# A decode step of gated attention and MLP: four groups of TensorE products turned from written-out code into loops with register addresses

## The chip, the cores and the metric

The kernel runs on one core of one Trainium2 chip. The metric is the device time of one execution in microseconds (us). Times of engine work below come from one profiled execution of the kernel, whose clock starts with the span. TensorE is called PE, and its weight loads PEld; VectorE is DVE, ScalarE ACT, GpSimd POOL, SyncE SP. Each engine has a sequencer that works through its own program in order. Instructions that the sequencer does itself (register arithmetic, branches, waits) are shown by the trace with their own names: FUSED_REGOPS, ALU_OP, MOVE, COMPARE_BRANCH, EVENT_SEMAPHORE.

## The reference

One token (x of 512 elements, bf16) goes through two branches, which are mixed by a gate:

```python
q = (x @ wq).reshape(B, Sq, H, Dh).transpose(0, 2, 1, 3)      # H = 32 heads, Dh = 128
scores = einsum("bhqd,bhkd->bhqk", q, k_cache) * (Dh ** -0.5)  # Sk = 65536 keys for each head
p = softmax(scores, axis=-1)
o = einsum("bhqk,bhkd->bhqd", p, v_cache)
a = o.transpose(0, 2, 1, 3).reshape(B, Sq, H * Dh) @ wo

b = (silu(x @ w_gate) * (x @ w_up)) @ w_down                   # 512 -> 1792 -> 512

g = sigmoid((x * gate_w).sum(-1, keepdims=True))
out = g * a + (1 - g) * b
```

K and V caches have 32 x 65536 x 128 bf16 elements each, 1074 MB together. All weights together are 14 MB.

## The kernel before

Every cache element is used once, so the kernel streams K and V through one large SBUF buffer `mem` (184 slots of 512 elements for each of the 128 partitions). For one head, K and V are each loaded in two halves (z = 0 and 1) of 8.39 MB. A partition holds R = 512 keys of a head.

**SP's queue (L214 to 252)** issues almost all loads, in an order written out by hand. Ahead of the block, wq and the weights of gate, up and down are issued (L205 to 207). Then come the two quarters of K's first half of head 0 (L221, 222). SP then waits for `s_q`, the end of the products with wq (L224), since the second half of K of head 0 goes into the slots of wq (V0). After that, for each head h: K's first half of head h once enough transposes are done (L227; for h = 1 eight of them, `NP`), V's first half of head h - 1 (for h = 1 after 13 transposes and after `s_b`, the end of the MLP's down product; later after a part of the V products), K's second half, V's second half. At the end come wo (L240) and the V of the last head in eight pieces (`tail`, L61: 128, 128, 128, 64, 32, 16, 12 and 4 rows), each with a semaphore `dt_[n]` of its own, and two last parts of wo (L249, 250).

**DVE (L318 to 432)** first serves the small head of the computation: x transposed, q in the layout that the scores want (L377 to 382), and the MLP's activation up to `guT` (L383 to 389). Then it transposes K by 32 x 32 blocks into the two buffers of `kt` (`transposes`, L336; in the head loop L405 and L412), each transpose waiting for the scores that used the same buffer two before (`qkdone`). It also spreads the exponentials for the V products (`shuffle`, L345).

**ACT** does the exponentials (L307) and small copies; among them qcur (L289) and gcol (L291, `s_gc`), one behind the other.

**PE (L434 to 585)**, in order:

- x transposed by four products (L440).
- The products with wq (L444 to 447): for each of 32 heads four products over c accumulate one column of psM. The last one raises `s_q`.
- q spread by `sel` (L452), the gate's broadcast (L456).
- `mlp_up` (L467 to 478): it waits for `s_gc` and the gate's and up weights; for each of 14 columns j, four products with wg and four with wu, 112 in all. The last one raises `s_h`.
- The down product (L481 to 484, 14 products of 512 columns).
- The head loop `Fori(0, H)` (L494 to 536): scores of head i in pairs of transposed blocks, and between them the V products of head i - 1. `scores` (L458) is written for 32 products; `pieces` runs pairs in a loop over j with `ds(j * (2 * PR) + o, 4)` as output address, or once with fixed addresses.
- After the loop: `turn` (L487), then `piece(0)` (128 products of one column into psW, L544), the gathering of the heads' outputs (L554, oR by DVE at L426), 31 products with wo (L558 to 560, 512 columns each, into psY; the last raises `s_y`), `piece(1)`, four small products with `hot` (L567), `piece(2)` to `piece(7)`, the last raising `s_w`, and the last products of wo (L583). ACT's copy (L314) and two writes of 0.5 KB end the kernel.

In `piece`, the weights of a product are a row block `vt[:, r * Dh:(r + 1) * Dh]` and the moving operand is one column `pb[:, col]`. For the first piece, k_col[r] is r.

Of the kernel before, what the change touches and what calls it, by code (L numbers as in the profile page):

```python
# [15 lines left out]
ds = bass.DynSlice  # L16
# [5 lines left out]
def bass_gated_mix__mha_block_cached__swiglu_ffn__decode_kernel(  # L22
# [11 lines left out]
    out: bass.AP,  # L34
):
    _, H, S, Dh = A_k_cache.shape
    D = A_wq.shape[0]
    F = B_w_gate.shape[1]
    Dc = D // P
    FC = F // P  # L40
    R = S // P
# [12 lines left out]
    k_col = [256 * z + PR * k_order[z].index(r // PR) + r % PR for z in range(2) for r in range(HR)]  # L54
# [10 lines left out]
    with ExitStack() as ctx:  # L65
        def sb(name, shape, dt):
            return ctx.enter_context(nc.sbuf_tensor(name, shape, dt))

        def psum(name, shape, dt):
            return ctx.enter_context(nc.psum_tensor(name, shape, dt))  # L70

        def sem(name):
            return ctx.enter_context(nc.semaphore(name))
# [3 lines left out]
        psY = psum("psY", [P, 512], F32)  # L77
        psM = psum("psM", [P, 512], F32)
        psQ = psum("psQ", [P, 4, 128], F32)
        psT = psum("psT", [P, 512], F32)  # L80
        psW = psum("psW", [P, 512], F32)
# [7 lines left out]
        pb = sb("pb", [P, 512], BF16)  # L89
# [7 lines left out]
        xTb = sb("xTb", [P, 16], BF16)  # L97
# [7 lines left out]
        oR = sb("oR", [P, 32], BF16)  # L105
# [3 lines left out]
        def at(kb, n):  # L109
            return mem[:, kb * KB:kb * KB + n]  # L110
# [32 lines left out]
        s_h = sem("s_h")  # L143
# [45 lines left out]
        wq_ap = at(WQ, Dc * H * Dh).rearrange("p (c n) -> p c n", c=Dc)  # L189
# [3 lines left out]
        wo_ap = at(WO, 32 * D).rearrange("p (j n) -> p j n", j=32)  # L193
# [241 lines left out]
        def _(pe):  # L435
# [3 lines left out]
            for c in range(Dc):  # L439
                last = nc.tensor.matmul(psM[:, c:c + 1], xv[:, c, :], ones[0:1, 0:1], start=True, stop=True)  # L440
            last.then_inc(s_xT, 1)
            pe.wait_ge(s_xTb, 1)
            pe.wait_ge(d["wq"], 16)
            for h in range(H):  # L444
                for c in range(Dc):
                    last = nc.tensor.matmul(psM[:, 128 + h:129 + h], wq_ap[:, c, h * Dh:(h + 1) * Dh],  # L446
                                            xTb[:, c:c + 1], start=(c == 0), stop=(c == Dc - 1))
            last.then_inc(s_q, 1)
            pe.wait_ge(s_qTb, 1)
            pe.wait_ge(s_sel, 1)  # L450
            for je in range(4):
                last = nc.tensor.matmul(psQ[:, je, 0:H], sel[:, je, :], qTb[:], start=True, stop=True)  # L452
# [14 lines left out]
            def mlp_up():  # L467
                pe.wait_ge(s_gc, 1)
                pe.wait_ge(d["wg"], 16)
                pe.wait_ge(d["wu"], 16)  # L470
                for j in range(FC):
                    for w, o in ((wg_ap, 64), (wu_ap, 80)):
                        for c in range(Dc):
                            last = nc.tensor.matmul(psM[:, o + j:o + j + 1], w[:, c, :, j], xTb[:, c:c + 1],  # L474
                                                    start=(c == 0), stop=(c == Dc - 1))
                last.then_inc(s_h, 1)

            mlp_up()
            pe.wait_ge(d["wd"], 16)
            pe.wait_ge(s_gu, 1)  # L480
            for j in range(FC):  # L481
                last = nc.tensor.matmul(psY[0:1, :], guT[:, j:j + 1], wd_ap[:, j, :],
                                        start=(j == 0), stop=False)
# [10 lines left out]
            with nc.tensor.Fori(0, H) as i:  # L494
                n = i * (2 * NP)
# [42 lines left out]
            def piece(n):  # L538
                kb, r0, nr = tail[n]
                pe.wait_ge(dt_[n], 16)  # L540
                vt = at(kb, nr * Dh)
                for r in range(nr):
                    col = k_col[r0 + r]
                    last = nc.tensor.matmul(psW[:, 0:1], vt[:, r * Dh:(r + 1) * Dh], pb[:, col:col + 1],  # L544
                                            start=(r0 + r == 0), stop=(r0 + r == R - 1))
                return last

            pe.wait_ge(s_or, H)
            turn()
            pe.wait_ge(s_pba, H)  # L550
            piece(0)
            pe.wait_ge(s_A, 1)
            pe.wait_ge(s_b0, 5)
            nc.tensor.matmul(psQ[:, 0, 0:32], amat[:].rearrange("p h q -> p (h q)"), bmat[:],  # L554
                             start=True, stop=True).then_inc(s_R, 1)
            pe.wait_ge(s_oR, 1)
            pe.wait_ge(d["wo"], 16)
            for j in range(31):  # L558
                last = nc.tensor.matmul(psY[0:1, :], oR[:, j:j + 1], wo_ap[:, j, :], start=False, stop=(j == 30))
            last.then_inc(s_y, 1)  # L560
            piece(1)
            pe.wait_ge(s_yr, 1)
            pe.wait_ge(s_hot, 1)
            pe.wait_ge(s_zz, 1)
            zt = [psZ[32 * (c // 2):32 * (c // 2) + 2, 0:128] for c in range(4)]
            for c in (0, 2, 1, 3):
                nc.tensor.matmul(zt[c], hot[0:1, c % 2, :], yrow[0:1, 128 * c:128 * c + 128],  # L567
                                 start=(c % 2 == 0), stop=False)
            pe.wait_ge(s_pbz, H)
            piece(2)  # L570
            piece(3)
            piece(4)
# [5 lines left out]
            for e in range(2):  # L578
# [3 lines left out]
                for c in (0, 2, 1, 3):  # L582
                    last = nc.tensor.matmul(zt[c], w4[:, e, c % 2, :], w2_ap[:, e, c, :], start=False,  # L583
                                            stop=(e == 1 and c % 2 == 1))
# [29 lines left out]
```

## Time and profile before

| | |
|---|---|
| device time, median of 3 runs | 2518.57 us (2518.57 to 2519.21) |
| the profiled execution | 2518.66 us |
| its span | 2517.4 us |
| PE busy | 1675.3 us (67%), 21432 matmuls |
| PEld busy | 956.8 us (38%) |
| DVE busy | 1397.7 us (56%) |
| ACT, POOL busy | 65.6 us (3%), 26.8 us (1%) |
| granted TensorE clock, mean | 0.711 |
| DMA from HBM | 1087.77 MB |
| code loaded by queue q8 | 9 packets, 0.15 MB |

Busy shares are averages over the whole span; what decides is which wait ends last in a stretch. The chain of waits follows the work that ended last back from the last instruction. In a timeline row, the first number is the start, the second the time to the end of the group, and in brackets stands how long the engine had stood idle before and what ended that. In an answer for one source line, three numbers divided by strokes are the shortest, the median and the longest duration in ns, and PEldq stands for the sequencer of PE.

### The profile page before, as it was taken

How to read it: one execution, taken by the hardware profiler on the slowest of the kernel's cores; microseconds unless marked ns; L12 is line 12 of the kernel's file. 1: busy time of each engine (PE TensorE's matmuls, PEld its weight loads, DVE VectorE, ACT ScalarE, POOL GpSimd, SP SyncE). 2: the span in 40 equal slices, each digit the busy share in tenths (PEclk: the TensorE clock that was granted, in tenths of full speed). 3: DMA queues.
4: the chain of work that ended last, by engine and by line, in shares of the span. 5: the costliest groups of instructions: out<-in, count | busy, mean ns of one | idle time of the engine just before them, and what ended most of it. 6: DMA issues, size and time to landing. Idle time of an engine off the chain costs nothing.

```text
span 2517.4 us, 50622 instructions
## 1 busy us (share of the span) xinstructions
PE 1675.3 (67%) x21432; PEld 956.8 (38%) x21432; DVE 1397.7 (56%) x1631; ACT 65.6 (3%) x195; POOL 26.8 (1%) x83
## 2 busy tenths in 40 slices
PE   4566756667666577566676666766657756667667
PEld 3333333333433334333333333343333433333334
DVE  3764565554655645646456555465464564644653
ACT  0000000000000000000000000000000000000000
POOL 0000000000000000000000000000000000000000
PEclk8667767677677677676776767767767767677677
DMA  9999999999999999999999999999999999999999
GB/s 418 433 433 434 435 433 433 434 433 433 433 433 433 433 433 433 433 433 433 433 435 432 434 433 434 433 434 433 434 433 433 433 433 434 433 433 433 433 434 396
DMA packets 20474, 1087.97 MB, mean 432 GB/s; under 512 B 2282, under 2 KB 2668, under 8 KB 2924
## 3 DMA queue, kind: packets, MB, share of 16 engines
q1 hardware_dynamic: 20452, 1087.78, 99.9%
q8 instruction: 9, 0.15, 0.0%
q14 instruction: 5, 0.04, 0.0%
q10 hardware_dynamic: 8, 0.00, 0.0%
HBM read 1087.77 MB, written 0.00 MB: 432 GB/s over the span
## 4 chain that ended last, share of the span: by engine, by line
DMA 72%; PE 27%; DVE 0%; issue 0%; SPq 0%; ACT 0%
DMA mem<-in_A_v_cache_dram 70%; PE psO L515 27%; DMA mem<-in_A_k_cache_dram 2%; DMA mem<-in_A_wq_dram 1%; DVE kt L336 0%; PE psM L446 0%; SPq L247 0%; PE psZ L583 0%; PE psW L544 0%; ACT fin L314 0%
## 5 line engine op out<-in xcount | busy, mean ns | idle before, releaser
L462 PE MATMUL psS<-qcur,kt 128*128 128x4 bf16 x16384 | 573.7, 169 | 776.4 <-DVE kt L405 458.4
L515 PE MATMUL psO<-mem,pb 128*4 128x512 bf16 x3968 | 1033.6, 428 | 35.2 <-DMA mem<-in_A_v_cache_dram 35.2
L405 DVE STREAM_TRANSPOSE kt<-mem 128x2048 uint32<-128x2048 uint32 x248 | 551.2, 2280 | 571.9 <-DMA mem<-in_A_k_cache_dram 571.0
L462 PEld LDWEIGHTS psS<-qcur,kt 128*128 128x128 bf16 x16384 | 534.7, 106 | 852.4 <-issue 850.0
L412 DVE STREAM_TRANSPOSE kt<-mem 128x2048 uint32<-128x2048 uint32 x248 | 547.6, 2274 | 407.6 <-DMA mem<-in_A_k_cache_dram 407.6
L515 PEld LDWEIGHTS psO<-mem,pb 128*4 128x4 bf16 x3968 | 361.2, 93 | 666.2 <-issue 235.7
L345 DVE COPY pb<-pa 32x64 bf16<-32x64 bf16 x1024 | 233.5, 228 | 24.2 <-PE psO L515 9.5
L350 DVE TENSOR_REDUCE sm<-psS 128x1 f32<-128x512 f32 x32 | 22.1, 692 | 42.3 <-PE psS L462 42.3
L336 DVE STREAM_TRANSPOSE kt<-mem 128x2048 uint32<-128x2048 uint32 x16 | 35.4, 2277 | 16.9 <-DMA mem<-in_A_k_cache_dram 16.9
L280 POOL PARTITION_ALL_REDUCE sm<-sm x32 | 11.2, 351 | 2392.6 <-DVE sm L350 2392.6
L301 ACT ACTIVATE oTn<-psT,gcol 128x1 bf16<-128x1 f32 x31 | 8.2, 263 | 1063.2 <-PE psT L489 1063.2
L489 PE MATMUL psT<-unit,orow 4*128 4x1 f32 x256 | 33.5, 248 | 0.8 <-ACT orow L299 0.8
L299 ACT ACTIVATE orow<-psO,sm 4x512 f32<-4x512 f32 x31 | 21.0, 677 | 439.5 <-issue 439.5
L489 PEld LDWEIGHTS psT<-unit,orow 4*128 4x128 f32 x256 | 30.8, 186 | 1.9 <-ACT orow L299 1.3
L305 ACT ACTIVATE sm<-sm 128x1 f32<-128x1 f32 x32 | 6.5, 203 | 886.3 <-POOL sm L280 886.3
L307 ACT ACTIVATE pa<-psS,sm 128x512 bf16<-128x512 f32 x32 | 22.0, 687 | 1.0
L544 PE MATMUL psW<-pb,mem 128*128 128x1 bf16 x512 | 14.6, 165 | 7.6 <-DMA mem<-in_A_v_cache_dram 7.1
L544 PEld LDWEIGHTS psW<-pb,mem 128*128 128x128 bf16 x512 | 14.1, 102 | 8.7 <-issue 6.5
L282 POOL PARTITION_ALL_REDUCE sm<-sm x32 | 12.3, 383 | 36.4 <-ACT pa L307 36.4
L446 PE MATMUL psM<-xTb,mem 128*128 128x1 bf16 x128 | 3.6, 165 | 11.1 <-DMA mem<-in_A_wq_dram 11.1
L474 PE MATMUL psM<-xTb,mem 128*128 128x1 bf16 x112 | 6.9, 198 | 4.9 <-DMA mem<-in_B_w_up_dram 4.9
L432 DVE TENSOR_SCALAR w<-psW,sm 128x2 bf16<-128x2 f32 x1 | 0.2, 221 | 16.5 <-PE psW L544 16.5
(64 smaller groups left out, 63.1 us busy)
## 6 DMA issues: line engine op xcount, KB each, us to landing
mem<-in_A_v_cache_dram SPq DMA_DIRECT2D x3, 4096.0 KB, 29.4
mem<-in_A_k_cache_dram SPq DMA_DIRECT2D x2, 4096.0 KB, 38.8
mem<-in_A_wq_dram SPq DMA_DIRECT2D x1, 4096.0 KB, 12.6
mem<-in_A_wo_dram SPq DMA_DIRECT2D x1, 3968.0 KB, 37.0
mem<-in_A_v_cache_dram SPq DMA_DIRECT2D x1, 2048.0 KB, 32.9
mem<-in_B_w_gate_dram SPq DMA_DIRECT2D x1, 1792.0 KB, 16.4
mem<-in_B_w_up_dram SPq DMA_DIRECT2D x1, 1792.0 KB, 21.3
mem<-in_B_w_down_dram SPq DMA_DIRECT2D x1, 1792.0 KB, 25.1
```

Of the source, the lines that this page charges most:

```text
L282: nc.gpsimd.partition_all_reduce(Lt, rsum, P, RADD).then_inc(s_L, 1)
L299: nc.scalar.mul(orow[0:4, :], psO[0:4, :], Li[0:4, :]).then_inc(s_or, 1)
L307: nc.scalar.activation(pa[:], psS[:], ACT.Exp, bias=nbias, scale=SCALE, accum_out=rsum).then_inc(expdone, 1)
L336: nc.vector.transpose(kt[:, i % 2, :].rearrange("p (j r t) -> p r j t", j=2, t=32), src.rearrange("p (r j t) -> p r j t", j=2, t=32)).then ...
L345: last = nc.vector.tensor_copy(dst, sr)
L350: nc.vector.reduce_max(mxs, psS[:], AX_X).then_inc(s_mx, 1)
L405: nc.vector.transpose(kt[:, c % 2, :].rearrange("p (j r t) -> p r j t", j=2, t=32), src.rearrange("p (r j t) -> p r j t", j=2, t=32)).then ...
L412: nc.vector.transpose(kt[:, c % 2, :].rearrange("p (j r t) -> p r j t", j=2, t=32), src.rearrange("p (r j t) -> p r j t", j=2, t=32)).then ...
L462: last = nc.tensor.matmul(psS[:, o:o + 4] if j is None else psS[:, ds(j * (2 * PR) + o, 4)], ktb[b][:, je // 2, r, :, je % 2], qcur[:, je, ...
L489: last = nc.tensor.matmul(psT[:, 0:1], orow[0:4, i * Dh:(i + 1) * Dh], unit[0:4, i:i + 1], start=(i == 0), stop=(i == 3))
L515: last = nc.tensor.matmul(psO[0:4, :], pb[:, k_col[256 * z + r]:k_col[256 * z + r] + 4], vt[:, r * Dh:(r + 4) * Dh], start=(z == 0 and par ...
L544: last = nc.tensor.matmul(psW[:, 0:1], vt[:, r * Dh:(r + 1) * Dh], pb[:, col:col + 1], start=(r0 + r == 0), stop=(r0 + r == R - 1))
```

## The change

Four groups of PE products that Python wrote out one by one become loops of the PE sequencer. Inside a loop, the addresses come from registers (`ds(expression, size)`). The last products of a group stay written out (in the piece the first eight), because they carry the start or stop flags or the semaphore.

- wq: 7 turns of 4 heads (16 products each), then 4 heads written out.
- gate and up: 13 turns of one column j (8 products each), then the last column.
- the last V's first piece: 8 rows, then 15 turns of 8 rows. The other pieces stay written out.
- wo: 5 turns of 5 products, then 6 written out.

Number, order and operands of the products stay as they were; no load, wait or semaphore is added or moved.

```diff
-            for h in range(H):
+
+            def project(h):
                 for c in range(Dc):
-                    last = nc.tensor.matmul(psM[:, 128 + h:129 + h], wq_ap[:, c, h * Dh:(h + 1) * Dh],
+                    last = nc.tensor.matmul(psM[:, ds(h + 128, 1)], wq_ap[:, c, ds(h * Dh, Dh)],
                                             xTb[:, c:c + 1], start=(c == 0), stop=(c == Dc - 1))
+                return last
+
+            with nc.tensor.Fori(0, (H - 4) // 4) as i:
+                for h in range(4):
+                    project(i * 4 + h)
+            for h in range(H - 4, H):
+                last = project(h)
             last.then_inc(s_q, 1)
...
-                for j in range(FC):
+                def up(j):
                     for w, o in ((wg_ap, 64), (wu_ap, 80)):
                         for c in range(Dc):
-                            last = nc.tensor.matmul(psM[:, o + j:o + j + 1], w[:, c, :, j], xTb[:, c:c + 1],
-                                                    start=(c == 0), stop=(c == Dc - 1))
-                last.then_inc(s_h, 1)
+                            last = nc.tensor.matmul(psM[:, ds(j + o, 1)],
+                                                    w[:, c, :, ds(j, 1)].rearrange("p m a -> p (m a)"),
+                                                    xTb[:, c:c + 1], start=(c == 0), stop=(c == Dc - 1))
+                    return last
+
+                with nc.tensor.Fori(0, FC - 1) as j:
+                    up(j)
+                up(FC - 1).then_inc(s_h, 1)
...
+                def row(r, col):
+                    return nc.tensor.matmul(psW[:, 0:1], vt[:, ds(r * Dh, Dh)], pb[:, ds(col, 1)],
+                                            start=(isinstance(r, int) and r0 + r == 0),
+                                            stop=(isinstance(r, int) and r0 + r == R - 1))
+
+                first = 0
+                if n == 0:
+                    first = 8
+                    for r in range(first):
+                        row(r, k_col[r])
+                    with nc.tensor.Fori(0, nr // 8 - 1) as i:
+                        for r in range(8):
+                            row(i * 8 + (first + r), i * 8 + (first + r))
+                    return
                 for r in range(nr):
-                    col = k_col[r0 + r]
-                    last = nc.tensor.matmul(psW[:, 0:1], vt[:, r * Dh:(r + 1) * Dh], pb[:, col:col + 1],
-                                            start=(r0 + r == 0), stop=(r0 + r == R - 1))
+                    last = row(r, k_col[r0 + r])
                 return last
...
-            for j in range(31):
-                last = nc.tensor.matmul(psY[0:1, :], oR[:, j:j + 1], wo_ap[:, j, :], start=False, stop=(j == 30))
+
+            def fold(j, stop):
+                return nc.tensor.matmul(psY[0:1, :], oR[:, ds(j, 1)],
+                                        wo_ap[:, ds(j, 1), :].rearrange("p a n -> p (a n)"), start=False, stop=stop)
+
+            with nc.tensor.Fori(0, 5) as i:
+                for j in range(5):
+                    fold(i * 5 + j, False)
+            for j in range(25, 31):
+                last = fold(j, j == 30)
             last.then_inc(s_y, 1)
```

## The prediction

> **What bounds it now.** I read the page's DMA and chain parts first, then the chain in order of time, then the timeline of PE at both ends, then the register operations by line.
>
> ```profile
> HBM read 1087.77 MB, written 0.00 MB: 432 GB/s over the span
> DMA 72%; PE 27%; DVE 0%; issue 0%; SPq 0%; ACT 0%
> ```
>
> The DMA row of the slices is 9 throughout. All the caches must come in once, so the time is 1087.77 MB at this rate plus whatever time the DMA engines stand still. PE's 27% in the chain is the release of a V buffer, behind which another load is already running. An edit on PE costs nothing until it (a) makes SP issue a load after the queue has run dry, or (b) ends later than the last data. The question is how much room each of the four places has.
>
> The head, from the chain in order of time, and PE's timeline there:
>
> ```profile
> 13.48 3.57 PE psM L446 x128
> 17.06 48.92 DMA mem<-in_A_k_cache_dram
> 66.00 11.09 DVE kt L336 x5
> ...
> 23.04 6.85 PE L474 MATMUL psM<-xTb,mem 128*128 128x1 bf16 x112 [4.92 <-DMA mem<-in_B_w_up_dram]
> 31.42 5.02 PE L482 MATMUL psY<-mem,guT 128*1 128x512 bf16 x14 [1.53 <-DVE guT L389]
> 39.40 1.22 PE L462 MATMUL psS<-qcur,kt 128*128 128x4 bf16 x32 [2.96 <-DVE kt L336]
> ```
>
> The second half of K of head 0 (8.39 MB) is issued when s_q comes (17.06) and lands at 66.00. At 433 GB/s it takes 19.4 us, so its transfer begins at 46.6: s_q may come some 29 us later at no cost. The next load (K of head 1) waits for eight transposes and goes out at 55.56; it is needed when the queue runs dry at 66.0. The first packet of wq started 1.03 us after its issue (0.72 to 1.75), so the room is about 66 - 1 - 55.56 = 9 us.
>
> The tail, PE's timeline:
>
> ```profile
> 2485.32 3.51 PE L544 MATMUL psW<-pb,mem 128*128 128x1 bf16 x128 [2.02 <-DMA mem<-in_A_v_cache_dram]
> 2489.16 8.61 PE L559 MATMUL psY<-mem,oR 128*1 128x512 bf16 x31 [0.28 <-DVE oR L426]
> 2497.71 3.36 PE L544 MATMUL psW<-pb,mem 128*128 128x1 bf16 x128
> 2504.77 3.55 PE L544 MATMUL psW<-pb,mem 128*128 128x1 bf16 x128 [3.17 <-DMA mem<-in_A_v_cache_dram]
> 2509.58 1.81 PE L544 MATMUL psW<-pb,mem 128*128 128x1 bf16 x62 [1.25 <-DMA mem<-in_A_v_cache_dram]
> 2511.89 1.21 PE L544 MATMUL psW<-pb,mem 128*128 128x1 bf16 x34 [0.50 <-issue]
> 2513.39 0.59 PE L544 MATMUL psW<-pb,mem 128*128 128x1 bf16 x16 [0.29 <-DMA mem<-in_A_v_cache_dram]
> 2514.33 0.60 PE L544 MATMUL psW<-pb,mem 128*128 128x1 bf16 x16 [0.36 <-DMA mem<-in_A_v_cache_dram]
> ```
>
> From piece 2 on PE waits for data. The idle times add to 3.17 + 1.25 + 0.50 + 0.29 + 0.36 = 5.57 us; some 0.4 of it is the semaphores' own latency, so the room is 5.2 us. Anything beyond is added to the end.
>
> **The price of a register address.** The kernel already has PE loops, over j in the scores:
>
> ```profile
> L462 PEldq FUSED_REGOPS  x3584: 46/46/65, 39.3 to 2465.4; - x200
> ...
> L508 PEldq ALU_OP  x224: 32/32/32, 42.5 to 2465.5; - x112
> L508 PEldq COMPARE_BRANCH  x224: 76/208/243, 42.6 to 2465.6; - x112
> ```
>
> 224 turns of j hold 16 different output columns each, and 224 x 16 = 3584: one FUSED_REGOPS for each different address, shared by the four products that use it. From the records in order of time: with 8 queued instructions (four weight loads, four matmuls) between two of them, the next starts 78 ns after the last one ends; with none between register instructions the gap is 58 to 60 ns. So the sequencer does not get below about 46 + 58 = 104 ns for an address. With two queued instructions between, interpolation (58 + 2 x 20/8) gives 63, thus 109. I take 106. In the scores this hides: 46 + 78 = 124 ns for four products against 4 x 26.7 = 107 for written-out ones, 1.17 against 1.01 us for 32 in the timeline. In the new loops nearly every product has an address of its own. A turn ends with the ALU_OP (32), a gap of 60, the taken branch (209, not taken 76) and a gap of 58: 0.36 us. Whether each turn opens with one more register instruction (0.10 us, as L508 does for its waits) I leave to the upper end.
>
> **wq (L444 to 448).** 28 heads in 7 turns. A head has one output column and four weight addresses (c differs): 5 operations, 20 to a turn. 7 x (20 x 0.106 + 0.36) = 17.4 us, and 16 written-out products x 27 ns = 0.4; with the entry 0.15 the stage takes 18.0 in place of 3.55. s_q moves from 17.03 to about 31.5 (+14.5). SP's queue has only the load of K0's second half there: inside its 29 us of room, nothing is lost yet. DVE's copy of q, the four products of L452, the qd copies and ACT's gcol follow at their old distance (s_gc at 19.73 + 14.5 = 34.2).
>
> **Gate and up (L471 to 476).** Before, they began at 23.04, when wu landed; now at 34.3. A turn has 2 output columns and 8 weight addresses: 13 x (10 x 0.106 + 0.36) = 18.5 us, plus 8 written out at 61 ns = 0.5, entry and last latency 0.3: they end at U = 53.6 instead of 29.89. The products' own 61 ns lie under 106.
>
> **What that delays.** DVE does guT before the transposes, PE does L482 before the scores. guT ends at U + 1.4; two transposes fill kt; L482 ends at U + 6.55; the first scores take 1.2, so the third transpose starts at U + 7.85 and, at 2.22 us each, the eighth ends at U + 21.2 = 74.8 (before 55.54). K of head 1 is issued then, its first packet comes about 1 us later. The last packets of K0's second half start at 64.8, and I count the hole from 65.1 to 75.8: **+10.7 us** (10.1 with 104 ns, 13.5 with 109 ns and the extra operation). The V load behind it needs 13 transposes, at U + 32.3 = 85.9, while K of head 1 runs until about 95: covered. After that every load waits as before, and a full stream can't win time back.
>
> **Piece 0 of the last V (L538 to 546).** Eight rows written out (0.2), then 15 turns of 8 rows with two addresses each (weights at vt, column at pb): 15 x (16 x 0.106 + 0.36) = 30.8 us. 31.2 in place of 3.5: +27.6.
>
> **wo (L558 to 560).** Two addresses to a product, 212 ns, against 278 ns of PE (8.61/31): 5 turns take the sequencer 5 x (10 x 0.106 + 0.36) = 7.1 us, PE needs 25 x 0.278 = 6.9. I take +0.3 (0 to 0.9).
>
> Tail: 27.6 + 0.3 - 5.2 = **+22.7 us** (22.2 to 25). DVE's yrow, w4 and the last wo rows are ready long before PE gets there, so nothing more is late. The products left (piece 1, hot, pieces 2 to 7) follow back to back at 27 ns.
>
> **Code.** 399 written-out products become 38, and 37 in loop bodies, so fewer code fetches: q8 moved 9 packets, 0.15 MB; even all of it at 432 GB/s is 0.35 us. No gain is reachable there: the one long branch in the trace, 3137 ns at L528 (56.0), with a 16 KB packet beginning 0.7 us after, lies under the wait for K at 66.0. A shifted program can put one such 3.1 us on the path at L522 or in the tail: up to +3, none taken.
>
> Rule and row differ in one thing. The Trainium skill (Advanced Engine Details and Errata, Sequencer Loop) says that other engine instructions can be read and queued while a control instruction executes. By that rule address work would overlap the queueing and the loops would come near the scores' pace, which is the second rival below; the trace speaks against it, since products queued earlier do go on, but the first weight load behind a FUSED_REGOPS starts 50 ns after its end, never inside it.
>
> **Sum.** The profiled execution took 2518.66 us with a span of 2517.4; it stands 0.1 above the median 2518.57. 2518.66 + 10.7 + 22.7 = 2552.1. Its own range is 2550 to 2560: 32.3 to 38.5 by the two ends above, and 3 for a code fetch.
>
> **Rivals.**
> 1. Cheap addresses: the two addresses of a row come out of one register instruction, or of a plain ALU_OP. One instruction of about 60 ns (118 with its gap) for a row of piece 0: 15 x (8 x 0.118 + 0.36) = 19.6, D = 16.6, tail +11.4; four for a head and eight for a turn of the up loop: U = 48.7, head +5.8: 2536. With ALU_OP (36 + 58 = 94 ns): +7.3 and +19.5: 2545. For it: L501's waits add three terms in one operation. Against: one operation for each single address at L462. Chance 0.10.
> 2. Not slower. The sequencer runs ahead of PE and the room takes the rest. In the head, s_q can slip 3.3 us before the wait for wu gives way (23.04 - 19.73), and U 13 (U + 21.2 may reach 65.1 - 1.0, so U up to 42.9): 16 us over 216 looped products, 75 ns each. In the tail 5.2 us over 145, 36 ns each. Below these prices nothing is lost. At the extra of the scores, 5 ns for a product, it is 1.2 and 0.7 us: 2518.7. For it: the scores' loops. Against: their addresses are shared by four. Chance 0.05.
> 3. Head or tail alone: the head's chain is shorter than I read it, since the queue still had work: 2518.66 + 22.7 = 2541. Chance 0.05.
> 4. Dear addresses: each takes two operations (0.2 us): U = 79.8, head +37, tail +50: 2606. Or a loop's body straddles a code block and each return fetches anew: 15 x 2.8 in piece 0, +42: 2594. The skill (Runtime: NRT & Kernel Launch, Instruction fetch mechanics) says that a taken branch out of the loaded window forces a fetch; here the h loop's return, over a far longer body, took 209 ns. Chance 0.08.
>
> The forecast has 0.72. The range 2536 to 2562 leaves out rivals 2 and 4 (0.13) and some of the forecast's own high end. About 0.2%, 5 us, is what a measurement of this kernel can tell: slower 0.94, same 0.05, faster 0.01, since nothing reachable is removed.
>
> **What would show it.** Right: wq's products spread over 18 us, gate and up over 19; the first scores at about 60; a hole of 10 us in DMA after 65; K of head 1 issued at about 75; piece 0 over 31 us with 240 register instructions at its line, and no DMA wait in PE between it and the end. Register spacing below 60 ns, or no hole in DMA, would make it wrong.

## The result and the profile after

The changed kernel takes 2562.9 us (median of 5 runs, 2561.65 to 2563.23) against 2519.05 us before (5 runs): 43.85 us more, ratio 1.0174, 95% interval 1.0163 to 1.0185. The profiled execution has a span of 2560.3 us. The prediction's sum was 2552.1, with a range of 2536 to 2562.

The pages' DMA parts, with the transfer rate in 40 equal slices of the span, here first the line of the kernel before and then, in slices of 64 us, those of the changed kernel:

```profile
GB/s 418 433 433 434 435 433 433 434 433 433 433 433 433 433 433 433 433 433 433 433 435 432 434 433 434 433 434 433 434 433 433 433 433 434 433 433 433 433 434 396
...
GB/s 414 329 440 428 440 428 440 427 437 431 429 439 427 441 427 438 430 438 430 438 429 434 434 431 437 427 441 427 437 431 437 431 435 432 434 433 432 436 427 217
...
q8 instruction: 7, 0.11, 0.0%
...
HBM read 1087.77 MB, written 0.00 MB: 425 GB/s over the span
```

Two slices fall out, the second (329) and the last (217; it was 396 before). The bytes are the same, so the loss lies in two places, and the heads between run at the old rate. PE's queue for code (q8) loaded 7 packets in place of 9.

The first place, in the timeline of all engines (rows picked; start, time to the group's end, and in brackets the idle time before):

```profile
34.76 43.72 SPq L218 DMA_DIRECT2D mem<-in_A_k_cache_dram  x2
...
37.70 1.15 PE L482 MATMUL psM<-xTb,mem 128*128 128x1 bf16 x8 [1.88 <-ACT gcol L291]
39.16 1.17 PE L482 MATMUL psM<-xTb,mem 128*128 128x1 bf16 x8 [0.32 <-issue]
...
58.59 4.50 DVE L336 STREAM_TRANSPOSE kt<-mem 128x2048 uint32<-128x2048 uint32 x2
58.83 5.09 PE L495 MATMUL psY<-mem,guT 128*1 128x512 bf16 x14 [1.53 <-DVE guT L389]
63.86 2.00 PE L470 MATMUL psS<-qcur,kt 128*128 128x4 bf16 x64
64.85 30.82 DVE L336 STREAM_TRANSPOSE kt<-mem 128x2048 uint32<-128x2048 uint32 x14 [1.76 <-PE psS L470]
```

SP issues two loads in the first row: K's second half of head 0 at 34.76 (17.06 before), when wq is done, and K of head 1 at 34.76 + 43.72 less its own 0.33, at 78.15 (55.56 before). Gate and up end at 57.3 (29.9 before), DVE transposes only after guT, PE starts the scores at 63.86 (39.40 before). In the records of the DMA packets none of a load starts between 65.0 and 79.1: a hole of 14.1 us. Counting bytes moved (each packet's bytes spread evenly over its time), the data are 15.5 to 15.8 us later than before from there on, to the end. That is more than the hole, because the transfer also runs thin around it: 108 GB/s in the last us before, and 218, 348, 348 and 399 in the four us behind, against 424 to 433 on either side.

The second place, PE's timeline at the end:

```profile
2500.80 2.28 PE L557 MATMUL psW<-pb,mem 128*128 128x1 bf16 x16 [1.11 <-DMA mem<-in_A_v_cache_dram]
...
2535.09 1.94 PE L557 MATMUL psW<-pb,mem 128*128 x8 [0.46 <-issue]
2537.22 0.19 PE L580 MATMUL psQ<-bmat,amat 128*128 128x32 bf16 x1 [0.19 <-issue]
2538.00 6.24 PE L586 MATMUL psY<-mem,oR 128*1 x20 [0.59 <-DVE oR L426]
...
2550.93 6.98 PE L557 MATMUL psW<-pb,mem 128*128 128x1 bf16 x256
2557.84 0.85 PE L617 MATMUL psZ<-mem,w 128*2 128x128 bf16 x8
```

Piece 0 starts 15.5 us later (2500.80 against 2485.32) and lasts to 2537.0, 36.2 us in place of 3.5. The waits for data that stood before pieces 2 to 7 are gone: their 256 products run in one stretch of 6.98 us. The last packet of the stream started at 2530.65; PE alone sets the end.

The register operations, by line:

```profile
L447 PEldq FUSED_REGOPS  x133: 42/46/79, 13.6 to 33.8; - x133
L451 PEldq FUSED_REGOPS  x7: 78/78/83, 13.4 to 31.3; - x7
L482 PEldq FUSED_REGOPS  x91: 46/46/79, 37.7 to 56.3; - x91
L487 PEldq FUSED_REGOPS  x13: 78/78/78, 37.6 to 55.3; - x13
L557 PEldq FUSED_REGOPS  x120: 46/74/84, 2501.1 to 2536.6; - x120
L557 PEldq ALU_OP  x105: 32/32/36, 2501.3 to 2536.8; - x105
L566 PEldq FUSED_REGOPS  x15: 78/78/84, 2500.9 to 2534.8; - x15
```

With wq there are 140 for 7 turns, the 20 a turn of the prediction. Gate and up have 104 for 13 turns, 8 and not 10: there an operation of 78 or 79 ns serves two addresses. Piece 0 has 240 for 15 turns, the 16 of the prediction. The instruction that opens each turn (L451, L487 and L566, 78 ns) is one of these and not one more. The counts were nearly right; the distances were not. Two rows of piece 0 in the trace's records (start in us, ns):

```
2516.148 LDWEIGHTS     105
2516.201 FUSED_REGOPS   74
2516.333 ALU_OP         32
2516.393 LDWEIGHTS     106
2516.446 FUSED_REGOPS   74
2516.578 ALU_OP         32
2516.638 LDWEIGHTS     102
```

A row takes 245 ns: 74, a gap of 58 with nothing queued between, 32, and a gap of 81 in which one weight load and one matmul are handed over. Some single gaps are longer (0.10 to 0.23 us). In the loops of wq and of gate and up, a 46 ns operation and a gap of 78 make 124 ns for a product.

### The profile page after: what moved, and what is told of

It reads as the page before. It is cut to its first block, busy times and chain, and to the rows that moved or that the text cites. A ratio compares the mean times of both kernels' runs of the same rounds, so it can differ in the third digit from the quotient of the medians.

```text
span 2560.3 us, 51240 instructions
## 1 busy us (share of the span) xinstructions
PE 1709.1 (67%) x21432; PEld 976.9 (38%) x21432; DVE 1397.2 (55%) x1631; ACT 65.6 (3%) x195; POOL 26.8 (1%) x83
## 4 chain that ended last, share of the span: by engine, by line
DMA 73%; DVE 14%; issue 10%; PE 3%; DVEq 0%; ACT 0%
DMA mem<-in_A_k_cache_dram 72%; DVE kt L405 7%; DVE kt L412 6%; PE psW L557 1%; DMA mem<-in_A_v_cache_dram 1%; PE psM L447 1%; PE psM L482 1%; DVE kt L336 0%; DMA mem<-in_A_wq_dram 0%; PE psY L586 0%; PE psY L495 0%; DVEq L410 0%; DVE qd L380 0%; DVEq L403 0%; PE psS L470 0%
## 5 line engine op out<-in xcount | busy, mean ns | idle before, releaser
L557 PE MATMUL psW<-pb,mem 128*128 128x1 bf16 (+1 forms) x512 | 30.6, 165 | 17.1 <-issue 7.1
L280 POOL PARTITION_ALL_REDUCE sm<-sm x32 | 11.2, 351 | 2408.0 <-DVE sm L350 2408.0
L557 PEld LDWEIGHTS psW<-pb,mem 128*128 128x128 bf16 (+1 forms) x512 | 22.9, 102 | 25.2 <-issue 13.2
L447 PE MATMUL psM<-xTb,mem 128*128 128x1 bf16 x128 | 16.5, 181 | 15.8 <-DMA mem<-in_A_wq_dram 11.3
L447 PEld LDWEIGHTS psM<-xTb,mem 128*128 (+1 forms) x128 | 12.2, 104 | 20.2 <-issue 18.1
L482 PE MATMUL psM<-xTb,mem 128*128 128x1 bf16 x112 | 15.7, 216 | 5.8 <-issue 3.9
```

Of the source, the lines that this page charges most:

```text
L447: last = nc.tensor.matmul(psM[:, ds(h + 128, 1)], wq_ap[:, c, ds(h * Dh, Dh)], xTb[:, c:c + 1], start=(c == 0), stop=(c == Dc - 1))
L482: last = nc.tensor.matmul(psM[:, ds(j + o, 1)], w[:, c, :, ds(j, 1)].rearrange("p m a -> p (m a)"), xTb[:, c:c + 1], start=(c == 0), stop= ...
L557: return nc.tensor.matmul(psW[:, 0:1], vt[:, ds(r * Dh, Dh)], pb[:, ds(col, 1)], start=(isinstance(r, int) and r0 + r == 0), stop=(isinsta ...
```

## The experiments

Each kernel was timed beside the kernel before on the same chip (2518.8 to 2518.9 us there). The theory from the traces: PE's sequencer pays for each register address; in the head this delays K of head 1 past its room, in the tail it delays the end; and what fits into the room costs nothing.

**The two places apart.** In the first kernel the piece and wo are written out again, in the second wq, gate and up:

```diff
-                if n == 0:
+                if n < 0:
...
-            with nc.tensor.Fori(0, 5) as i:
...
+            for j in range(31):
```

> Loops for wq and for gate and up only; the last V's first piece and wo are written out. Theory (PE's sequencer pays for each register address, in two separate places; the head makes a hole in the DMA stream, the tail delays the end): 15.5 us over before, about 2534.5, with the hole of 14 us after 65 us and PE waiting for data again in the tail, as before. Rival A (the head's delay is absorbed over 31 heads and all of the loss is in the tail): about 2519.

> Loops for the last V's first piece and wo only; wq, gate and up are written out. Theory: 27.4 us over before, about 2546.5, no hole in DMA after 65 us, piece 0 over 36 us. Rival A (all of the loss is in the tail): about 2563.

Measured 2534.82 (16.0 over before, ratio 1.0063, interval 1.0047 to 1.008) and 2547.18 (28.4 over, 1.0112, 1.0095 to 1.0129). Together 44.4, against 43.85 for both in one kernel: the two add up, and rival A falls. With the head loops alone the packets show the hole (14.7 us from 64.8), and PE waits for data in the tail as it did before:

```profile
2520.74 3.55 PE L557 MATMUL psW<-pb,mem 128*128 128x1 bf16 x128 [1.99 <-DMA mem<-in_A_v_cache_dram]
2525.55 1.87 PE L557 MATMUL psW<-pb,mem 128*128 128x1 bf16 x64 [1.26 <-DMA mem<-in_A_v_cache_dram]
```

**The head's room.** One of the two head loops alone, then both with only 4 columns of gate and up in the loop:

```diff
-                with nc.tensor.Fori(0, FC - 1) as j:
+                with nc.tensor.Fori(0, 4) as j:
                     up(j)
+                for j in range(4, FC - 1):
+                    up(j)
```

> Loop for wq only. Theory: s_q comes some 17.7 us later, but inside its room; gate and up end at about 44.5, K of head 1 is issued at about 65.3, some 1 to 2 us too late: 2519.5 to 2521. Rival B (a late s_q itself costs time, since the load behind it is late; or every loop's excess goes to the end): 10 to 17 us over before, 2529 to 2536.

> Loop for gate and up only. Theory: they start at 23.0 as before and end at about 43, K of head 1 is issued at about 63.7, just in time: 2519 to 2520, so that the two head loops alone cost 0 to 2 us together and 15 in one kernel. Rival B (every loop's excess goes to the end): 10 to 13 us over before, 2529 to 2532.

> As the kernel with the two head loops alone, but only 4 columns of gate and up go through the loop. Theory: gate and up end at 48.9 in place of 57.5, K of head 1 is issued at about 69.7, the hole is 8.5 us shorter: 2526.3. Rival B (excess times add up without room): the loop of wq with its 17.7 us alone gives 2535 or more.

Measured 2522.1 (3.3 over; 1.0013, 1.0003 to 1.0022), 2520.11 (1.3 over; 1.0006, 0.9996 to 1.0016) and 2525.86 (7.1 over; 1.0027, 1.0017 to 1.0038). Alone the loops cost 3.3 and 1.3 us (the second cannot be told from nothing), together 16.0: the excess does not add up, it is cut off at a room, so rival B falls. The lateness of the data behind the pause, by bytes moved, is in each of these kernels what its profiled run lost: 15.8 to 16.0 us with both loops (15.9 over before), 7.3 to 7.6 with 4 columns (7.4), 1.8 to 2.0 with wq alone (2.1) and 1.6 to 1.7 with gate and up alone (1.4). The loop of wq alone, timeline:

```profile
34.75 30.14 SPq L218 DMA_DIRECT2D mem<-in_A_k_cache_dram  x2
```

s_q is as late as with both loops (34.75), yet K of head 1 goes out at 64.6, not 78, and the pause between packets is 2.2 us, not 14.1. So it is not the late load behind s_q that costs. The median of the kernel with wq's loop alone was 1 us dearer than expected. Its profiled run (2520.85, the fastest of ten) lies within what was expected, and no trace shows what the other nine lost. In that trace PE stands still 0.98 us inside piece 3, in the middle of its products; the trace of the kernel before has such a stop of 0.50 us too (the row at 2511.89 in the prediction), and more of them follow below.

**The price of an address and of a turn.** In the changed kernel, one address of a row is fixed; or the turns of the piece are made three times as long:

```diff
-                            row(i * 8 + (first + r), i * 8 + (first + r))
+                            row(i * 8 + (first + r), first + r)
```

```diff
-                    with nc.tensor.Fori(0, nr // 8 - 1) as i:
-                        for r in range(8):
-                            row(i * 8 + (first + r), i * 8 + (first + r))
+                    with nc.tensor.Fori(0, (nr - 8) // 24) as i:
+                        for r in range(24):
+                            row(i * 24 + (first + r), i * 24 + (first + r))
```

> The changed kernel, but in the first piece's loop the column of pb has a fixed address: all 15 turns use the columns 8 to 15 (so the rows 16 to 127 are weighted with other rows' values). One address for a row in place of two. Theory (a register instruction with products between two of them costs its own 46 ns and a gap of 78): a row falls from 245 to 124 ns and a turn from 2.40 to 1.49 us, 13.6 us less than the changed kernel: 2549.3. Rival D (the loop's turn or the weight load from a register address is what costs): no more than 3 us less, 2560 or over.

> The changed kernel, but the first piece's loop has 5 turns of 24 rows in place of 15 turns of 8. Theory: ten turns' ends are saved, 0.44 us each, the addresses stay: 4.4 us less than the changed kernel, 2558.5. Rival D (the turn is what costs): 24 us less, 2539.

Measured 2550.74 and 2558.17: 12.2 and 4.7 us less than the changed kernel's 2562.9 (each ratio against before: 1.0128, 1.0111 to 1.0145, and 1.0157, 1.014 to 1.0174). From return to return a turn takes 1.64 us with one address, 2.41 with two, and 6.43 with 24 rows. Rival D falls on both: ten returns saved make only 4.7 us, one address less in each of 120 rows makes 12.2. The first kernel gave less than expected since its one operation grew to 64 ns (142 a row, not 124).

**wo's share.** Only the piece is a loop:

> Loop for the last V's first piece only. Theory: wo's loop is hidden under PE's own 512-column products but for some 0.8 us, so about 26.6 us over before: 2545.5. Rival C (wo's loop has a larger share, since its products also take two register instructions each): 2538 to 2542.

Measured 2545.47 (26.6 over; 1.0105, 1.0088 to 1.0122), 1.7 below the kernel with wo's loop as well (2547.18), so rival C falls. How large wo's share is can't be told closely. The four runs of the piece alone lie 1.6 us apart, so that their median meets the expected 2545.5 more closely than they allow to claim. Between the two traces PE's rows with wo, first looped and then written out, differ by 0.7 us in length and 0.3 in the wait before them:

```profile
2522.48 9.76 PE L574 MATMUL psY<-mem,oR 128*1 x31 [0.59 <-DVE oR L426]
...
2522.10 9.08 PE L574 MATMUL psY<-mem,oR 128*1 128x512 bf16 x31 [0.28 <-DVE oR L426]
```

But the 31 products take 8.1 to 9.7 us in the nine traces in which they are written out, and 9.2 to 9.8 in the five with the loop. So the 25 looped products come under PE's own 512-column work nearly whole.

**The tail's room.** Only 2 or 5 turns of the piece are looped, the rest is written out:

```diff
-                    with nc.tensor.Fori(0, nr // 8 - 1) as i:
+                    with nc.tensor.Fori(0, 2) as i:
                         for r in range(8):
                             row(i * 8 + (first + r), i * 8 + (first + r))
+                    for r in range(first + 8 * 2, nr):
+                        row(r, k_col[r])
```

> Only 16 rows of the last V's first piece go through a loop (2 turns of 8), all other products are written out. Theory: piece 0 takes 2 x 2.41 + 0.15 - 16 x 0.027 = 4.5 us longer, PE has 5.2 us of waiting for data behind it: 2518.8 to 2519.5. Rival E (there is no room in the tail, each us of PE goes to the end): 2523.3.

> 40 rows of the first piece go through the loop (5 turns), all other products are written out. Theory: 5 x 2.41 + 0.15 - 40 x 0.027 = 11.1 us longer, less 5.2 of room: 2524.7. Rival E: 2530.

Measured 2520.67 (1.9 over; 1.0008, 0.9999 to 1.0017) and 2524.1 (5.3 over; 1.002, 1.0011 to 1.003). The second agrees with 5.2 us of room within 0.6, and rival E (2530) falls there. The first lies between the theory (0 to 0.7 over) and rival E (4.5 over), and its trace says why, PE's timeline:

```profile
2505.41 1.69 PE L545 MATMUL psW<-pb,mem 128*128 128x1 bf16 x60
2508.66 3.55 PE L545 MATMUL psW<-pb,mem 128*128 128x1 bf16 x128 [1.55 <-issue]
2514.86 1.95 PE L545 MATMUL psW<-pb,mem 128*128 128x1 bf16 x68 [2.65 <-issue]
```

PE stops in the middle of written-out code, at no wait, after 60 products of piece 2 and again after exactly 128 more, which with their weight loads are 256 instructions. Code packets of 16 KB run at those times (2506.31 to 2507.38 and 2512.41 to 2513.53), and PE goes on 1.28 and 1.33 us after each has ended. The next kernel moves the code and not the data: 9 columns of gate and up become a loop too, in the head's room, which shortens the program ahead of the tail.

> The kernel with 2 turns in the first piece, and 9 columns of gate and up in a loop too, which costs nothing by itself and makes PE's program some 115 instructions shorter ahead of the tail. Theory F (in the tail of the kernel with 2 turns PE stood still 1.7 and 2.8 us for the next 16 KB of its own code, 60 products into piece 2 and 128 products later): the standstills move with the code by some 57 products, to about product 118 of piece 2 and of the products behind it, while the waits for data stay; 2518.8 to 2521. Rival G (a piece of data was late there): the standstills stay 60 products into piece 2, 2520.7.

Measured 2519.45 (1.0002, 0.9993 to 1.0012):

```profile
2505.77 3.25 PE L552 MATMUL psW<-pb,mem 128*128 128x1 bf16 x119
2511.21 3.57 PE L552 MATMUL psW<-pb,mem 128*128 128x1 bf16 x128 [2.19 <-issue]
2514.94 0.40 PE L552 MATMUL psW<-pb,mem 128*128 128x1 bf16 x9 [0.15 <-issue]
```

The stop moved from product 60 to product 119, with the code (57 were expected, 59 came). So it is the code that is late, and with one such stop nearly gone (0.15 us) the 2 turns fit into the room but for 0.6 us. In the tails of all traces there are nine such stops, the one in the kernel before among them, and each ends 1.26 to 1.39 us after a 16 KB packet of q8.

**Loops only where they are covered:** 9 columns of gate and up, and wo.

> Loops only where work covers them: 9 columns of gate and up, and wo; wq, five columns of gate and up and the first piece are written out. Theory: gate and up end at 39.1, wo's loop takes under 1 us more than written out, both inside their room: 2518.6 to 2519.4, no difference from before. Rival B: 6 us over, 2525.

Measured 2518.87 against 2518.8 (1.0000, 0.9991 to 1.0009), with a trace of 8 code packets in place of 9. No kernel was faster than before: the DMA stream is full but for its first and last few us, and nothing here shortens these.

## Why the prediction was right or wrong

**The mechanism was right, place by place.** The loss sits where it was put: a hole in the DMA stream because K of head 1 waits for eight transposes, behind guT and the down product; and PE's own length after piece 0, with the waits before pieces 2 to 7 used up. s_q being late cost nothing by itself, wo's loop was nearly covered, and the stages between did not change. The direction was right; the size was short by a quarter, 33.4 of 43.85.

**The step that failed is the price of a register address.** The prediction took 106 ns, from a gap of 58 ns with nothing between two register instructions and 78 with eight queued ones, and set about 63 for two by interpolation. The gap with two queued instructions is 78 to 81, the same as with eight. So an address with its product takes 124 ns in wq and in gate and up. In piece 0 a row takes 245 ns for its two addresses and not 212: 19 of the 33 ns come from the gaps (58 + 81 against 2 x 60) and 14 from the operations (74 + 32 against 2 x 46). The upper end was therefore too low as well. Term by term:

| term | predicted | measured |
|---|---|---|
| a turn of wq's loop | 2.48 us | 2.98 |
| end of wq's products, s_q | 31.5 | 34.7 |
| a turn of gate and up | 1.42 | 1.48 |
| their end U | 53.6 | 57.3 |
| K of head 1 issued | 74.8 | 78.15 |
| loss in the head | 10.7 | 16.0 (head loops alone) |
| a row of piece 0, and a turn | 0.212, 2.06 | 0.245, 2.41 |
| piece 0 | 31.2 | 36.2 |
| wo's loop | 0.3 | 1.7 between medians, 1.0 between traces |
| loss in the tail | 22.7 | 28.4 (tail loops alone) |

Of the 3.7 us by which U came late, 3.2 are wq's (its turn is 0.50 us longer than predicted). Sixteen gaps of 78 in place of 60 ns make 0.29 of that 0.50, and four operations of 78 or 79 in place of 46 ns another 0.13; the rest are mostly single longer gaps. The extra register instruction in a turn, which the prediction left to its upper end, did not come: the one that opens a turn is among the 20 and the 16 that were counted. Gate and up need 8 operations in a turn and not 10, so that their turn came out nearly right (1.42 against 1.48 us) by two errors that cancel, which is luck.

A second term was left out in the head. The prediction counted the hole from packet start to packet start, 10.7 us. It was 14.1 in the changed kernel, since U was late, but the data are 15.5 to 15.8 us late behind it, because the transfer also runs thin around the hole. With the head loops alone the hole is 14.7, the data are 15.8 to 16.0 late and the time is 16.0 longer.

In the tail, one of the five idle times that the prediction took for waits for data (0.50 us at 2511.89, released by "issue") is a stop for code. The 0.4 us that it took off for the semaphores' latency is shown by no run. With 5 turns piece 0 was 10.7 us longer (2485.59 to 2499.84 in its trace) and the time 5.3, which puts the room near 5.4, but the spread of wo's products is as large as such differences.

**The rivals.** Cheap addresses: two addresses in one operation do occur (gate and up), but not for the rows of the piece. Its U of 48.7 does not come out of its own prices: 106 to 118 ns for each operation give 47.8 to 50.4, and so 2535 to 2538 in place of 2536. Not slower: its reasoning holds where there is room, as the loops in room, 9 columns and wo, show. Head or tail alone: the head loops alone cost 16.0 us and the tail loops alone 28.4, so both count. Dear addresses and a fetch at every return did not happen: a row of piece 0 took one operation of 74 and one of 32 ns for its two addresses, and the returns took 207 to 229 ns, at a loop's end once 83 or 76.

**The rule weighed there.** The Trainium skill (Advanced Engine Details and Errata, Sequencer Loop) lets other engine instructions be queued while a control instruction executes. The trace shows no such overlap for the instructions behind one: the first weight load starts 48 to 50 ns after the end of a FUSED_REGOPS and 28 or 29 after an ALU_OP, and PE's products follow the register instructions one by one, 124 or 245 ns apart.

The code fetches were named (up to 3 us, none taken), and in the changed kernel none shows: after the stream had ended, code packets came every 3.3 to 3.7 us and the 256 last products ran without a stop. In the kernel with 2 turns they decided a us or two.

## What to carry to other kernels

A loop on PE with a register address for nearly every product runs at the sequencer's pace, here 124 ns for one address and 245 ns for two, against 27 ns for a written-out product of one column; products of 512 columns (278 ns) cover it, and four products on one address nearly do (124 ns against 107 written out). Whether that costs anything is decided by the room of the wait behind it: find the next load that PE's end releases and the time at which the queue runs dry, and add up all that shares this room before changing it in pieces, since two loops that cost 3.3 and 1.3 us alone cost 16.0 together. When the queue has run dry, the loss is the pause and the thin transfer around it, here 1.2 to 1.5 us more with both head loops.

## What the runs showed of the hardware that was not expected

The gap between two register instructions on PE's sequencer has two common values: 58 to 60 ns with nothing between them, 78 to 81 with one pair or four pairs of weight load and matmul between.

Written-out code has a price of its own while the DMA queues are full. In the tail with 2 looped turns, 256 instructions ran in 3.55 us, but PE could go on only 6.2 us after the block had begun (2508.66 to 2514.86): stops of 1.55 and 2.65 us. With the stream ended, the 256 products of pieces 2 to 7 ran without one, in 6.91 to 6.99 us: in the changed kernel and in four others, and in the kernel with 5 turns, where the stream ended 1.1 us into them. Why the code comes later beside the stream is not shown: the packets themselves took 1.0 to 1.1 us beside the stream and 0.9 to 1.4 behind it. The Trainium skill (Runtime: NRT & Kernel Launch, Instruction fetch mechanics) calls the crossing of a 16 KiB boundary mostly hidden; here that holds with idle DMA queues and not with full ones.
